# The last steps of the weight pieces, queued one by one on GpSimd ahead of the diagonal

## The chip, the core and the metric

The kernel runs on one core of one Trainium2 chip. The metric is the device time of the run in microseconds, lower is better. A core has five engines with a queue of their own each: TensorE (PE, matrix products), VectorE (DVE), ScalarE (ACT), GpSimd (POOL) and SyncE (SP, which issues the transfers here). Each engine works through its queue in the order in which the program issued it; between engines there are semaphores.

## The reference

Attention that keeps the 32 largest scores of each row, and behind it a two-layer block with a sigmoid-gated activation:

```python
B, H, S, D = 8, 8, 576, 64
scores = scale * np.matmul(q, k.transpose(0, 1, 3, 2))
kth = np.partition(scores, -32, axis=-1)[..., -32:-31]
scores = np.where(scores >= kth, scores, -1e9)
attn = softmax(scores)                    # with 1e-9 added to the sum
x = (attn @ v) -> (B*S, H*D)              # 4608 x 512
h = x @ w_in                              # 512 x 2048
out = (h / (1 + np.exp(-1.702 * h))) @ w_out   # 2048 x 512
```

`q`, `k`, `v` are float32. The two weight matrices are float64, and the kernel makes float32 of them on the chip.

## The kernel before

**Slots.** The attention is cut into `N` slots, 18 for each of the 8 batches: 128 query rows of two heads at a time (and slots for the rows left over). `slots` lists them. For a slot, TensorE makes scores (`scores`, L237), ScalarE copies them to SBUF (`copy_scores`, L248), VectorE finds the 32 largest of each row in four rounds of MAX8 (L257) and MATCH_REPLACE8 (L260) for each of two heads (`topk`, 14 operations). GpSimd makes the threshold `cut` (L276) and the shift `low` (L277) from it (`bounds`); ScalarE masks (L285) and takes exponentials (L288), whose sums are `den`. VectorE adds 1e-9 (`some`, L297) and takes the reciprocal (`rden`, L299). TensorE turns the probabilities round (`turn`, L319 and L322, later L317), ScalarE copies the result (`pt`, L327), TensorE multiplies by the values (L350).

**The division.** In the first eleven slots (`n < SETTLED`, 11) GpSimd writes a diagonal matrix `by` of the reciprocals (L303, two operations of 128x128), and the turn multiplies by it, so it divides on the way. `by` has one buffer (`dgp`): the diagonal of the next slot waits until the last turn that reads the one before is through. Later slots scale the probabilities themselves, one head on ScalarE (L305) and one on GpSimd (L306).

**The block behind.** 128 finished rows go through `hidden` (L400, with `win`), `tanh` (L417), `gate` (L433 on VectorE in the first slots, L430 and L431 on GpSimd later) and `project` (L448, with `wout`), which is issued from slot 8 on.

**The weights.** There are 32 pieces of 128x512 numbers, 16 of `w_in` and 16 of `w_out`. They come in during the first slots: 2 pieces belong to slots 0 and 1, 3 to each of slots 2 to 9, 2 to slots 10 and 11 (`by_slot`). Transfers into 8 buffers (`raws`) bring the float64 numbers as pairs of 32-bit words. Five steps make float32 of a piece: `size` (ScalarE, L147), `shift` (VectorE, L148), `low` (ScalarE, L150), `sign` (ScalarE, L149), and on GpSimd an integer addition (L143) and a multiplication by the sign (L144), called `finish`. `size`, `shift`, `low` and `sign` run in the piece's own slot; `finish` is put on the list `unfinished`, and `finish_one` issues it in the next slot.

**The order of the work.** The engines' queues are written by hand (`tc.manual_schedule()`): the order of the Python calls is the order on each engine. In `slot(n)` GpSimd gets `bounds(n - 1)`, then, between the operations of `topk(n)`, the entries of `unfinished` and `by` of slot n - 1 (`divide(n - 1)`, after the sixth operation of top-k). The turn of slot n - 1 is issued in slot n from `TURNS` (4) on; in slots 2 to 4 the turn of slot n - 2 is issued at the slot's start. From slot 12 on `two_slots` takes two slots at a time, and `find` issues one entry of `unfinished` after each operation of top-k from the third on. The list `finished` holds one entry for each finished piece, and `project` is issued only when its pieces are on it.

In the text a slot's number is the `n` of `slot(n)`, from 0; "the turn" is L319 and L322; "piece" is the GpSimd part of a piece (L143 and L144) where GpSimd's queue is spoken of.

Of the kernel before, what the change touches and what calls it, by code (L numbers as in the profile page):

```python
# [9 lines left out]
ALU = mybir.AluOpType  # L10
# [3 lines left out]
I32 = mybir.dt.int32  # L14
# [14 lines left out]
def kernel(  # L29
# [27 lines left out]
    nc = tc.nc  # L57
# [24 lines left out]
    TURNS = 4  # L82
# [44 lines left out]
    def round_piece(n):  # L127

        c, g = pieces[n]
        dst = wout[:, g, :] if c is None else win[:, c, g * PIECE : (g + 1) * PIECE]
        words = raw.pop(n)[:].rearrange("p (n w) -> p n w", w=2)
        low, high = words[:, :, 0], words[:, :, 1].bitcast(F32)
        bits, whole = dst.bitcast(U32), dst.bitcast(I32)  # L140

        def finish():
            nc.gpsimd.tensor_tensor(out=whole, in0=whole, in1=low.bitcast(I32), op=ALU.add)  # L143
            nc.gpsimd.tensor_tensor(out=dst, in0=dst, in1=high, op=ALU.mult)  # L144

        return {
            "size": lambda: nc.scalar.activation(dst, high, AF.Abs, scale=REBASE),  # L147
            "shift": lambda: nc.vector.tensor_scalar(bits, bits, 3, None, op0=ALU.logical_shift_left),  # L148
            "sign": lambda: nc.scalar.activation(high, high, AF.Sign),  # L149
            "low": lambda: nc.scalar.mul(out=low.bitcast(I32), in_=low, mul=2.0**-29),  # L150
            "finish": finish,
        }


# [89 lines left out]
    def copy_scores(n):  # L244
        ps = st[n].pop("ps")
        sc = st[n]["sc"] = scp.tile([P, 2, S], F32, name="sc")
        for i in range(2):
            nc.scalar.copy(out=sc[:, i, :].rearrange("p (c k) -> p c k", c=2), in_=ps[i][:, :, 0:HALF])  # L248

    def topk(n):  # L250

        sc = st[n]["sc"]
        top = st[n]["top"] = small.tile([P, 2, TOPK], F32, name="top")
        left = lefts.tile([P, 2, S], F32, name="left")

        def largest(r, i):
            nc.vector.max(top[:, i, 8 * r : 8 * r + 8], (left if r else sc)[:, i, :])  # L257

        def remove(r, i):
            nc.vector.match_replace(  # L260
                left[:, i, :], top[:, i, 8 * r : 8 * r + 8], (left if r else sc)[:, i, :], LOWEST
            )

        ops = []
        for r in range(TOPK // 8):
            ops += [lambda r=r, i=i: largest(r, i) for i in range(2)]
            if r < TOPK // 8 - 1:
                ops += [lambda r=r, i=i: remove(r, i) for i in range(2)]
        return ops

    def bounds(n):

        top = st[n]["top"]
        cut = st[n]["cut"] = small.tile([P, 2], F32, name="cut")
        low = st[n]["low"] = small.tile([P, 2], F32, name="low")
        nc.gpsimd.tensor_scalar(cut[:], top[:, :, TOPK - 1], -1.0, None, op0=ALU.mult)  # L276
        nc.gpsimd.tensor_tensor(out=low[:], in0=top[:, :, TOPK - 1], in1=top[:, :, 0], op=ALU.subtract)  # L277

    def exponentials(n, between=lambda: None):

        sc, cut, low = st[n]["sc"], st[n]["cut"], st[n]["low"]
        pr = st[n]["pr"] = prp.tile([P, 2 * S], F32, name="pr")
        den = st[n]["den"] = small.tile([P, 2], F32, name="den")
        for i in range(2):
            nc.scalar.activation(sc[:, i, :], sc[:, i, :], AF.Prelu, bias=cut[:, i : i + 1], alpha=HUGE)  # L285
        between()
        for i in range(2):
            nc.scalar.activation(  # L288
                pr[:, i * S : (i + 1) * S], sc[:, i, :], AF.Exp, bias=low[:, i : i + 1],
                accum_out=den[:, i : i + 1],  # L290
            )

    def divide(n):

        den, pr = st[n]["den"], st[n]["pr"]
        some = small.tile([P, 2], F32, name="some")
        nc.vector.tensor_scalar_add(some[:], den[:], 1e-9)  # L297
        rden = small.tile([P, 2], F32, name="rden")
        nc.vector.reciprocal(rden[:], some[:])  # L299
        if n < SETTLED:  # L300
            by = st[n]["by"] = dgp.tile([P, 2, P], F32, name="by")
            for i in range(2):
                nc.gpsimd.tensor_scalar(by[:, i, :], ident[:], rden[:, i : i + 1], None, op0=ALU.mult)  # L303
        else:
            nc.scalar.activation(pr[:, 0:S], pr[:, 0:S], AF.Copy, scale=rden[:, 0:1])  # L305
            nc.gpsimd.tensor_scalar(pr[:, S : 2 * S], pr[:, S : 2 * S], rden[:, 1:2], None, op0=ALU.mult)  # L306
# [22 lines left out]
    def turn_main(n):  # L329
        for i in range(2):  # L330
            turn(n, i * NF, MAIN[i], NF)

    def turn_ends(n):

        turn(n, 2 * NF, FULL, 1)
# [76 lines left out]
    def tanh(aside):  # L412

        if to_gate:
            ph, g, rows = to_gate.pop()
            th = thp.tile([P, G, P], F32, name="th")
            nc.scalar.activation(th[:], ph[:], AF.Tanh, scale=0.851 / RAISE)  # L417
            if aside:
                h = raws.tile([P, G, P], F32, name="h", tag="raw")
                nc.scalar.copy(out=h[:], in_=ph[:])  # L420
                ph = h
            gated.append((th, ph, g, rows))
# [65 lines left out]
    unfinished = []  # L488
    early = []
    finished = []  # L490

    def finish_one():
        unfinished.pop(0)()
        finished.append(None)

    def may_project(waiting):

        return len(to_project) > waiting and len(finished) >= NG * CC + (to_project[0][1] + 1) * G
# [63 lines left out]
    def bring_all():  # L562

        waiting = len(ready)
        while put_off:
            put_off.pop(0)()
        if len(ready) > waiting:
            hidden()

    def slot(n):  # L570

        todo = later.pop(n, [])
        for fn, args in todo:
            if fn is not prepare:
                fn(*args)
        preparing = [args for fn, args in todo if fn is prepare]
        some = [round_piece(x) for x in by_slot.get(n, [])] if n else early
        if n == 0:
            for piece in some:
                piece["low"]()  # L580
                piece["sign"]()
        else:
            bounds(n - 1)

            exponentials(n - 1, bring_all if n % 4 == 1 else lambda: None)
            copy_scores(n + 1)
            bring_all()
            while signs:
                signs.pop(0)()
            if 1 < n <= TURNS:  # L590
                turn_main(n - 2)
                turn_ends(n - 2)
            for piece in some:
                piece["size"]()
            tanh(False)
        for i, op in enumerate(topk(n)):
            op()
            if i == 2:
                for _ in range(min(1, len(unfinished))):
                    finish_one()  # L600
            if i == 5:
                if n > 0:
                    divide(n - 1)
                while unfinished:
                    finish_one()
            if i == 10:
                gate(False)
        for piece in some:
            piece["shift"]()
            unfinished.append(piece["finish"])  # L610
        if n < NP:
            for args in preparing:
                prepare(*args)
        if n >= TURNS:
            turn_main(n - 1)
            turn_ends(n - 1)
        if n > 0:
            for piece in some:
                piece["low"]()
        scores(n + 2)  # L620
        if n == SETTLED:
            copy_scores(n + 2)
        if n == 0:
            return
        for i, piece in enumerate(some):
            if n == TURNS and i > 0:
                signs.append(piece["sign"])
            else:
                piece["sign"]()
        idle = not ready and n < TURNS  # L630
        if 1 < n <= TURNS:
            values(n - 2, put_off if n == TURNS else None)
        if n >= TURNS:
            values(n - 1, put_off)
        if n >= NP:
            for args in preparing:
                prepare(*args)
        if n > PROJECTS and may_project(2):
            project(range(G))
        if idle:  # L640
            stay_warm(8)
        hidden()
# [118 lines left out]
```

## Time and profile before

| | |
|---|---|
| median of 4 runs | 1612.61 us (1612.29 to 1613.07) |
| the profiled execution | 1612.37 us |
| its span | 1610.6 us |
| PE busy | 1577.9 us (98%) |
| DVE busy | 1477.4 us (92%) |
| ACT busy | 1151.5 us (71%) |
| POOL busy | 745.8 us (46%) |
| one MAX8 or MATCH_REPLACE8, 128x576 | 743 to 747 ns |
| `raw` transfer, 512 KB | 3.4 and 5.1 us from issue to landing |

The page cuts the span into 40 slices of 40 us; a digit is an engine's busy share in tenths, and in the row PEclk the clock that TensorE was granted. The chain of waits follows the work that ended last back to the start, at each step to what released it. In timelines a row is the start, the duration, the engine, the line, the operation, what is written from what, and how many; in brackets the idle time of the engine before it and what ended it. Rows of like instructions are merged (x3), and a VectorE instruction's start there overlaps the end of the one before by about 0.08 us.

Two waits of TensorE in the first 110 us:

| row of the timeline | idle before, ended by |
|---|---|
| L319 at 59.60 us | 0.77 us, POOL `by` |
| L319 at 107.16 us | 2.60 us, POOL `by` |

### The profile page before, as it was taken

The page shows a single profiled execution, that of the slowest core. Times are in us where ns is not written, and L with a number is a line of the kernel's source. Part 1 is how long each engine was busy: PE and PEld are TensorE (multiplying, and loading weights), DVE is VectorE, ACT ScalarE, POOL GpSimd, SP SyncE. Part 2 cuts the span into 40 slices and gives each one's busy share as a digit, 9 for nine tenths or more (in the row PEclk, how much of TensorE's full clock was granted, in tenths as well). Part 3 has the DMA queues.
Part 4 walks back from the last instruction along what each step waited for, and adds up shares of the span by engine and source line. Part 5 has one row for each costly group of instructions (what it writes and reads, how often), then busy time and mean ns, then how long its engine had stood idle before and what let it go on. Part 6 is the DMA issues. An engine that isn't in the chain of part 4 may idle for free.

```text
span 1610.6 us, 32158 instructions
## 1 busy us (share of the span) xinstructions
PE 1577.9 (98%) x12045; PEld 1181.1 (73%) x12045; DVE 1477.4 (92%) x3218; ACT 1151.5 (71%) x2442; POOL 745.8 (46%) x780
## 2 busy tenths in 40 slices
PE   7789999999999999999999999999999999999999
PEld 5667777777777777777777777777777777777776
DVE  7999999999999989999999999999999999999960
ACT  7898776777776776677766777677767777777751
POOL 3877334444444434444444434444444444444430
PEclk8899999999999999999999999999999999999999
DMA  7451111010001001110001000001000100000000
GB/s 225 139 154 46 33 30 29 19 38 5 23 15 45 22 23 30 30 43 16 22 15 45 22 23 25 22 20 38 15 22 16 44 22 23 23 8 8 8 8 14
DMA packets 99100, 56.61 MB, mean 35 GB/s; under 512 B 81536, under 2 KB 90240, under 8 KB 98944
## 3 DMA queue, kind: packets, MB, share of 16 engines
q1 hardware_dynamic: 98512, 54.25, 12.1%
q8 instruction: 95, 1.56, 0.4%
q14 instruction: 61, 0.50, 0.1%
q10 hardware_dynamic: 432, 0.30, 0.1%
HBM read 45.09 MB, written 9.44 MB: 34 GB/s over the span
## 4 chain that ended last, share of the span: by engine, by line
PE 92%; DVE 6%; ACT 1%; issue 0%; POOL 0%; ACTq 0%; POOLq 0%
PE ph L400 32%; PE po L448 31%; PE s_ps L237 9%; PE o L350 9%; PE tp L317 8%; DVE top L257 3%; DVE left L260 2%; PE tp L205 2%; ACT sc L248 1%; PE tp L319 1%; DVE win L148 1%; PE none L165 0%; PE tp L211 0%; DVE wout L148 0%; ACT pr L305 0%
## 5 line engine op out<-in xcount | busy, mean ns | idle before, releaser
L257 DVE MAX8 top<-left 128x8 f32<-128x576 f32 x864 | 609.3, 747 | 0.0
L448 PE MATMUL po<-wout,gT 128*128 128x512 f32 x1152 | 540.2, 593 | 0.7 <-ACT ob L453 0.7
L400 PEld LDWEIGHTS ph<-xT,win 128*128 128x128 f32 x4096 | 467.8, 192 | 41.5 <-issue 41.0
L400 PE MATMUL ph<-xT,win 128*128 128x128 f32 x4096 | 484.6, 277 | 0.1
L260 DVE MATCH_REPLACE8 left<-top,left 128x576 f32<-128x576 f32 x576 | 423.4, 743 | 0.0
L306 POOL TENSOR_SCALAR pr<-pr,rden 128x576 f32<-128x576 f32 x133 | 229.5, 1726 | 349.9 <-ACT th L417 345.5
L448 PEld LDWEIGHTS po<-wout,gT 128*128 128x128 f32 x1152 | 197.9, 191 | 146.3 <-issue 144.6
L327 ACT COPY pt<-tp 128x512 f32<-128x512 f32 (+1 forms) x432 | 192.7, 481 | 150.6 <-PE tp L317 142.7
L430 POOL TENSOR_SCALAR th<-th 128x512 f32<-128x512 f32 x131 | 195.7, 1494 | 220.8 <-ACT th L417 220.8
L285 ACT ACTIVATE sc<-sc,cut 128x576 f32<-128x576 f32 x288 | 208.2, 774 | 120.6 <-POOL cut L276 118.6
L248 ACT COPY sc<-s_ps 128x576 f32<-128x576 f32 x288 | 169.8, 644 | 70.0 <-PE s_ps L237 69.7
L288 ACT ACTIVATE pr<-sc,low 128x576 f32<-128x576 f32 x288 | 219.2, 764 | 0.0
L317 PEld LDWEIGHTS tp<-ident,pr 128*128 128x128 f32 x1197 | 143.1, 141 | 102.0 <-issue 57.4
L260 DVE MATCH_REPLACE8 left<-top,sc 128x576 f32<-128x576 f32 x288 | 211.6, 742 | 0.0
L257 DVE MAX8 top<-sc 128x8 f32<-128x576 f32 x288 | 202.0, 743 | 2.2 <-ACT sc L248 2.2
L237 PE MATMUL s_ps<-k_t,q_t 64*128 64x288 f32 (+1 forms) x1280 | 182.2, 431 | 0.3 <-ACT k_t L207 0.3
L317 PE MATMUL tp<-ident,pr 128*128 128x128 f32 x1197 | 174.2, 273 | 0.0
L431 POOL TENSOR_TENSOR gT<-th,h 128x512 f32<-128x512 f32 x131 | 167.0, 1275 | 10.9
L350 PE MATMUL o<-pt,v_l 128*64 128x128 f32 (+1 forms) x2560 | 157.7, 266 | 0.7
L350 PEld LDWEIGHTS o<-pt,v_l 128*64 128x64 f32 x2560 | 130.4, 137 | 32.4 <-ACT pt L327 13.5
L237 PEld LDWEIGHTS s_ps<-k_t,q_t 64*128 64x128 f32 (+1 forms) x1280 | 99.4, 178 | 58.9 <-issue 41.4
L276 POOL TENSOR_SCALAR cut<-top 128x2 f32<-128x2 f32 x144 | 38.0, 264 | 206.8 <-DVE top L257 206.8
(66 smaller groups left out, 1174.3 us busy)
## 6 DMA issues: line engine op xcount, KB each, us to landing
q_l<-in_q_dram SPq DMA_DIRECT2D x64, 128.0 KB, 3.1
raw<-in_moe_w_in_dram SPq DMA_DIRECT2D x16, 512.0 KB, 5.1
v_l<-in_v_dram SPq DMA_DIRECT2D x32, 256.0 KB, 3.0
raw<-in_moe_w_out_dram SPq DMA_DIRECT2D x16, 512.0 KB, 3.4
out_dram<-ob SPq DMA_DIRECT2D x32, 256.0 KB, 2.3
k_l<-in_k_dram SPq DMA_DIRECT2D x62, 128.0 KB, 3.0
ends<-in_q_dram SPq DMA_DIRECT2D x32, 32.0 KB, 2.7
v_e<-in_v_dram SPq DMA_DIRECT2D x64, 16.0 KB, 2.5
```

Source lines behind the costliest of these rows:

```text
L237: nc.tensor.matmul(ps[i][rows, c, 0:HALF], lhsT=qT[b, hps[p]][on, cols], rhs=kT[b, hps[p]][on, FIRST[i] + c * HALF : FIRST[i] + (c + 1) * ...
L257: nc.vector.max(top[:, i, 8 * r : 8 * r + 8], (left if r else sc)[:, i, :])
L260: nc.vector.match_replace(left[:, i, :], top[:, i, 8 * r : 8 * r + 8], (left if r else sc)[:, i, :], LOWEST)
L285: nc.scalar.activation(sc[:, i, :], sc[:, i, :], AF.Prelu, bias=cut[:, i : i + 1], alpha=HUGE)
L288: nc.scalar.activation(pr[:, i * S : (i + 1) * S], sc[:, i, :], AF.Exp, bias=low[:, i : i + 1], accum_out=den[:, i : i + 1],)
L306: nc.gpsimd.tensor_scalar(pr[:, S : 2 * S], pr[:, S : 2 * S], rden[:, 1:2], None, op0=ALU.mult)
L317: nc.tensor.transpose(tp[:, c * P : (c + 1) * P], pr[:, at], ident[:])
L327: nc.scalar.copy(out=to, in_=tp[:, 0 : blocks * P])
L350: nc.tensor.matmul(o[j * D : (j + 1) * D, 0 : cols.stop - cols.start], lhsT=main[:, j, c, :] if c < NF else tail[:, j, :], rhs=pt[:, j * N ...
L400: nc.tensor.matmul(ph[:, i, :], lhsT=win[:, c, f * P : (f + 1) * P], rhs=xT[:, c, :], start=(c == 0), stop=(c == CC - 1),)
L430: nc.gpsimd.tensor_scalar(th[:], th[:], 1.0, None, op0=ALU.add)
L448: nc.tensor.matmul(po[:], lhsT=gT[:, i, :], rhs=wout[:, f, :], start=(f == 0), stop=(f == FC - 1))
```

## The change

Each piece leaves two entries on `unfinished` instead of one, the addition and the multiplication, and `finish_one` issues one of them. The count on `finished` moves into the multiplication. Ahead of `divide(n - 1)`, after the third operation of top-k, up to three entries are issued in slots 4 and on, and up to six in slots before; it was one piece, that is one addition and one multiplication, in every slot. What is left of the list follows `divide` as before. `find` is not edited; as it issues one entry per operation of top-k, in slot 12 it now issues three operations ahead of `divide` and one behind it, where it was two pieces ahead of it.

```diff
@@ round_piece
+        def add():
+            nc.gpsimd.tensor_tensor(out=whole, in0=whole, in1=low.bitcast(I32), op=ALU.add)
+
         def finish():
-            nc.gpsimd.tensor_tensor(out=whole, in0=whole, in1=low.bitcast(I32), op=ALU.add)
             nc.gpsimd.tensor_tensor(out=dst, in0=dst, in1=high, op=ALU.mult)
+            finished.append(None)
...
-            "finish": finish,
+            "finish": [add, finish],
@@ finish_one
     def finish_one():
         unfinished.pop(0)()
-        finished.append(None)
@@ slot
             if i == 2:
-                for _ in range(min(1, len(unfinished))):
+                for _ in range(min(3 if n >= TURNS else 6, len(unfinished))):
                     finish_one()
             if i == 5:
                 if n > 0:
                     divide(n - 1)
...
             piece["shift"]()
-            unfinished.append(piece["finish"])
+            unfinished.extend(piece["finish"])
```

## The prediction

> **What bounds the kernel now.** I read the shares of the chain of waits first, then the chain in order of time, then GpSimd's and VectorE's timelines in the first 110 us, then the granted clock in short windows. The profiled execution took 1612.37 us (span 1610.6).
>
> ```profile
> POOL 3877334444444434444444434444444444444430
> PEclk8899999999999999999999999999999999999999
> ...
> PE 92%; DVE 6%; ACT 1%; issue 0%; POOL 0%; ACTq 0%; POOLq 0%
> ```
>
> GpSimd (POOL), the only engine whose order changes, has no share of the chain. The 6% of VectorE (DVE) are all at the front. There the chain reads (start, duration, what):
>
> ```profile
> 40.00 1.00 DVE win L148 x3
> ...
> 50.91 2.61 DVE win L148 x3
> ...
> 63.44 2.63 DVE win L148 x3
> ...
> 76.62 1.40 DVE win L148 x3
> ...
> 88.53 1.43 DVE wout L148 x3
> ...
> 100.52 1.45 DVE wout L148 x3
> ...
> 106.50 0.61 POOL by L303
> 107.11 0.04 issue
> 107.16 3.68 PE tp L319 x16
> 110.84 0.37 PE tp L322 x4
> ```
>
> The reader should see one step with five prices. Three `shift`s (L148) cost 1.00 us at the end of slot 2 and 2.61, 2.63, 1.40, 1.43 and 1.45 at the ends of slots 3 to 7. Everything between them is top-k without a pause. At 107.16, in slot 8, the chain goes over to TensorE, which from 200 us on has no gap at all. So whatever the front gains or loses until 107.16 arrives whole at the end. GpSimd shows what makes the dear shifts:
>
> ```profile
> 46.38 1.18 POOL L303 TENSOR_SCALAR by<-ident,rden 128x128 f32<-128x128 f32 x2 [2.52 <-PE tp L322]
> ...
> 50.17 1.30 POOL L143 TENSOR_TENSOR win<-win,raw 128x512 int32<-128x512 int32 x1
> 51.55 1.35 POOL L144 TENSOR_TENSOR win<-win,raw 128x512 f32<-128x512 f32 x1
> 52.88 0.68 POOL L276 TENSOR_SCALAR cut<-top 128x2 f32<-128x2 f32 x1
> ```
>
> In slot 3 GpSimd waits 2.52 us for `by`'s buffer, and so its last piece still runs when the shifts begin at 50.84. The first shift ends at 51.76, 0.28 after the addition's end (51.48), the second at 53.19, 0.29 after the multiplication's end (52.90). A shift that meets a two-input GpSimd operation waits it out. `cut` is queued behind the same piece and comes 2 us after top-k's end at 50.91, and ScalarE's exponentials wait for it.
>
> **The change, part by part.** No instruction is added or taken away. The orders of TensorE, VectorE, ScalarE and SP stay, and with them every DMA issue. On GpSimd `by` (L303) moves behind its slot's second piece in slots 1 and 2 and behind all three in slot 3, and in slots 4 to 11 behind one more addition. In slot 12 the last multiplication goes behind the scaling of `pr` (L306).
>
> Slots 1 and 2: the second piece moves into the wait ahead of `by` (1.60 and 2.65 us). GpSimd was idle before `cut` here already (1.73 and 0.66), so nothing is gained. 0.
>
> Slot 3: additions and multiplications follow at 1.36 and 1.27 us (48.90 to 50.17), so a piece is 2.63. From 41.20 three end by 41.20 + 3 x 2.63 = 49.1, and `by` (1.18) by 50.3, before the shifts at 50.84. Their price falls from 2.61 to slot 2's 1.00: **-1.61**. `by` is 2.8 us later, but is read only by the turn at 51.92 in slot 4, 1.6 us on. Without that cover the excess would go onto ScalarE's copies, which wait for the turn.
>
> Slot 4: VectorE is 1.61 early throughout. `cut` is no longer late, and the exponentials start 1.11 after top-k's end (as 41.11 after 40.00), at 52.02 and not 53.59: 1.57 early. The turn whose end frees `by` follows them, so `by` starts at 58.95 - 1.57 = 57.38. Three operations are done by 56.0; the other three end 5.07 after `by`'s start (1.14 + 1.27 + 1.36 + 1.30), at 62.45. The first shift wants to start at 63.35 - 1.61 = 61.74 and still waits. At the end of slot 5 in the trace such a wait until 0.53 after the start made the price 1.40, 0.40 over; 0.71 makes it 1.58. **-1.05**.
>
> Slots 5 to 7: `by` waits for `rden`, with 1.85 to 2.04 us of idle time in front of it. One addition with its gap is 1.36 and fits. Three operations remain behind `by`: they end 5.07 after it, near 73.0 in slot 5, with top-k's end at 63.41 + 10.55 = 73.96. So each shift price falls to 1.00: **-0.40, -0.43, -0.45**. From slot 8 on the same happens beside a TensorE that is the bound: 0.
>
> Sum: 1.61 + 1.05 + 1.28 = 3.94 us by the start of slot 8's top-k. What ScalarE may keep back: its exponentials in slot 5 start 7.25 after slot 4's `by`, at 64.63, and their sums are there 3.26 later, at 67.89; VectorE wants them at 63.41 + 4.02 = 67.43 (70.09 less 66.07): 0.46 lost. `tanh` ends 7.64 after that start, at 72.27; the gate (L433) wants it at 71.6: 0.6 more. Together 1.1 us lost if TensorE's half clock in slot 4 stays as it is (59.5 to 62.8 at 0.50), about 0.1 if the earlier turn meets the full clock sooner. I take 0.2 to 0.3, because the 57.38 start leaves more busy time in the window before; both ends stay: 2.8 to 3.8. So **-3.7**.
>
> The small step `some` (L297) is the new meeting. In slots 1 to 11 it now comes up while a piece runs. Two rows show that:
>
> ```profile
> 153.64 0.70 DVE L297 TENSOR_SCALAR some<-den 128x2 f32<-128x2 f32 x1 [0.71 <-ACT pr L288]
> ...
> 184.03 0.50 DVE L297 TENSOR_SCALAR some<-den 128x2 f32<-128x2 f32 x1
> ```
>
> Alone it takes 0.15. At 153.64 a multiplication ran until 0.68 after its start; at 184.03 a one-input operation ran on for 1.36 and cost 0.35. In slots 2 to 7 it starts 4.68 (two pieces) or 5.02 (three) after the last top-k's end, and the second addition ends at 4.78 or 5.12: 0.1 later, about its own length. I take 0 each; the bounds are 0 and one more operation, 1.36.
>
> The Trainium skill, "SBUF — State Buffer", section "Who interferes with whom", speaks against the change: of a GpSimd and a two-port VectorE instruction the later one fully blocks until the first is through. Of the two rows 153.64 agrees; 184.03 does not, as `some` was done 1 us before the GpSimd operation. By the rule the sum would lose about 0.1 per slot, by the rows nothing.
>
> Slot 12: the multiplication (1.30) now stands between `pr` and the gate's two GpSimd steps (L430, L431). Before `cut` there was 0.93 idle, so `cut` is some 0.4 late. The `pr` that comes of it was scaled by 166.35 and is read by TensorE at 176.84, ten us on: 0. Without that cover, 0.4. The pieces' raw buffers come free up to 4 us earlier in slots 1 to 4 and 1.3 in later ones, so SP's loads behind them start no later: 0.
>
> **The clock at the hand-over.** TensorE ran slot 8's turn at half clock (PEclk in short windows; columns as in the page, PE first):
>
> ```profile
> 93.60:97.00 3.40, 1.80 (x16) 1.80 (x16) 3.37 (x9) 3.40 (x9) 2.44 (x3) 1.00 0.79 225
> 103.90:107.20 3.30, 0.70 (x7) 0.51 (x6) 3.27 (x11) 3.30 (x10) 1.29 (x3) 1.00 0.52 162
> 107.30:110.60 3.30, 3.30 (x16) 3.29 (x16) 3.30 (x8) 1.66 (x4) 3.22 (x4) 0.50 0.38 85
> ```
>
> A gap of 2.60 us before 107.16 left 0.70 busy in one window, and the next was at 0.50: the turn took 3.68 and not 1.79 as at 120.82. A gap of 1.75 (1.80 busy) kept the full clock. Slots of 11.55 instead of 11.95 make the gap about 2.2, between the two. The forecast keeps the half clock; the full one saves 1.89 more.
>
> The Trainium skill, "TensorE: Matmul & The Clock Gate", section "Why this matters for your kernels", asks for gaps of no more than about 3 us; by it slot 8 would not have been slow at all, which the 0.50 row contradicts. By the page the clock adds nothing to the sum; by the rows it adds up to 1.89.
>
> **The rivals.**
> *Full clock in slot 8:* 3.7 + 1.89 = 5.6 saved, 1606.8. For it: the shorter gap. Against: 2.2 is nearer to 2.60 than to 1.75.
> *ScalarE and the half clock keep more:* a slot with a half-clock turn goes from `by` to `by` in 11.99 (82.56 to 94.55), 0.44 over 11.55, whatever the shifts cost. With the 1.1 of slot 5 and two such slots, 3.94 - 1.1 - 0.88 = 2.0: 1610.4. For it: at 94.06 `some` waited for ScalarE already. Against: slots 5 and 7 ran at full clock.
> *No gain:* `by` still delays the last piece, or the shifts wait for something else: 1612.4. Against: the 0.28 and 0.29 us above.
> *Slower: `some` misses the gap between two operations* and is shut out for one more, 1.36, in each of slots 1 to 7: 9.5 lost, 3.9 gained, 1618. It decides from the third miss on (4.1). For it: in slots 1 to 3 a multiplication follows the addition at 0.07. Against: the shifts at 50.84 took just such a gap, and in slots 4 to 7 `by` follows, which itself waits for `some`.
>
> **How the numbers follow.** Forecast (0.45): 1612.37 - 3.7 = 1608.7; the median is 0.24 higher, inside the runs' spread of 0.8, so I leave it. Full clock 0.25; ScalarE 0.20; no gain 0.04; slower 0.06. The forecast's own range is 1608.3 to 1609.8 (3.8 and 2.8, with 0.3 of spread). The range goes from 1606.3 (5.6 and 0.5 of spread) to 1611.2, which leaves out no gain, slower and little else. 0.2%, which is about what a measurement can tell, lies at 1609.4. Faster: full clock and 0.42 of the forecast, 0.67; same: ScalarE, no gain and the forecast's last 0.03, 0.27; slower 0.06.
>
> **What would show it.** In the profile after: shifts of 1.00 at the ends of slots 3 and 5 to 7 and near 1.6 in slot 4; `by` with a wait for the turn left in slot 4 only; `cut` at top-k's end; slot 8's turn near 103.4; from there the same rows. A `some` over 0.3, a VectorE idle before `some` or the gate, or a slot 8 turn of 1.8 would each name the rival that came in.

## The result, and the profile after

| | before | after |
|---|---|---|
| median | 1612.46 us (54 runs, 1610.52 to 1613.81) | 1610.21 us (34 runs, 1608.00 to 1611.27) |
| the profiled execution | 1612.37 us, span 1610.6 | 1608.05 us, span 1606.2 |

By the medians 2.25 us are gained; the ratio of the times is 0.9983, with an interval of 0.9978 to 0.9988, which is 1.9 to 3.5 us. The 34 runs lie in groups: 7 between 1608.0 and 1608.6, 25 between 1609.9 and 1610.5, 2 near 1611.2. The profiled execution is one of the first group; a second profile (experiment `a1_again`, 1610.31 us) is of the large one. Both are read here.

VectorE's timeline of the changed kernel, the three shifts (now L151) at the ends of slots 3 to 7 (start, duration, engine, line):

```profile
50.44 1.08 DVE L151 TENSOR_SCALAR win<-win 128x512 uint32<-128x512 uint32 x3
...
61.34 1.39 DVE L151 TENSOR_SCALAR win<-win 128x512 uint32<-128x512 uint32 x3
...
73.84 1.08 DVE L151 TENSOR_SCALAR win<-win 128x512 uint32<-128x512 uint32 x3
...
85.36 1.08 DVE L151 TENSOR_SCALAR wout<-wout 128x512 uint32<-128x512 uint32 x3
...
96.86 1.07 DVE L151 TENSOR_SCALAR wout<-wout 128x512 uint32<-128x512 uint32 x3
```

These rows hold about 0.08 us that overlap the end of top-k. Without it the prices are 1.00, 1.31, 1.00, 1.00 and 0.99 us, where they were 2.61, 2.63, 1.40, 1.43 and 1.45. GpSimd's timeline of the same kernel shows why in slot 3:

```profile
47.39 1.30 POOL L146 TENSOR_TENSOR win<-win,raw 128x512 f32<-128x512 f32 x1
48.66 1.19 POOL L306 TENSOR_SCALAR by<-ident,rden 128x128 f32<-128x128 f32 x2
50.61 0.99 POOL L279 TENSOR_SCALAR cut<-top 128x2 f32<-128x2 f32 x1 [0.76 <-DVE top L260]
```

The last piece and `by` are done at 49.85, GpSimd waits 0.76 us for top-k, and `cut` starts with the shifts and not 2 us behind them. TensorE's timeline of the same kernel has what was not forecast:

```profile
91.63 2.87 PE L322 MATMUL tp<-by,pr 128*128 128x128 f32 x16 [2.36 <-POOL by L306]
...
103.14 2.05 PE L322 MATMUL tp<-by,pr 128*128 128x128 f32 x16 [1.34 <-POOL by L306]
105.64 0.44 PE L325 MATMUL tp<-by,pr 128*64 128x128 f32 x4 [0.45 <-ACT pt L330]
...
152.09 1.12 PE L451 MATMUL po<-wout,gT 128*128 128x512 f32 x2 [0.49 <-POOL wout L146]
```

Slot 8's turn (103.14) runs at the full clock; slot 7's, behind a gap of 2.36, now runs into the half clock (a window from 92.7 to 96.0 us stands at 0.50). At 152.09, in slot 12, TensorE waits for a multiplication of GpSimd.

Every profile of this study can be cut at three points: the first shift (end of slot 0's top-k), the start of slot 8's turn, and the product that follows the first output copy (L451, slot 12). What follows the last point is 1452.3 to 1452.4 us in all twelve, so a span is the sum of four numbers:

| profile | opening | front | middle | rest | span |
|---|---|---|---|---|---|
| before | 18.77 | 88.38 | 51.11 | 1452.32 | 1610.6 |
| after | 18.37 | 84.77 | 50.77 | 1452.33 | 1606.2 |
| `a1_again` (after) | 19.55 | 85.97 | 50.67 | 1452.33 | 1608.5 |
| `a2_first` | 19.28 | 86.78 | 50.89 | 1452.33 | 1609.3 |
| `a3_rest` | 18.97 | 87.30 | 51.81 | 1452.32 | 1610.4 |
| `a4_slot12` | 19.07 | 85.93 | 50.22 | 1452.35 | 1607.6 |
| `b1_fill4` | 19.32 | 84.29 | 51.06 | 1452.33 | 1607.0 |
| `b2_fillall` | 18.57 | 84.13 | 49.48 | 1452.34 | 1604.5 |
| `b3_fillbefore` | 18.68 | 88.23 | 51.13 | 1452.35 | 1610.4 |
| `b4_some` | 18.39 | 88.22 | 50.82 | 1452.34 | 1609.8 |
| `c1_four` | 19.29 | 84.02 | 49.51 | 1452.37 | 1605.2 |
| `c2_fillall` | 19.68 | 84.13 | 49.50 | 1452.33 | 1605.6 |

The opening is the same code in all of them and differs by up to 1.3 us. So the front and the middle are what the experiments are compared by, beside the medians.

### The profile page after: what moved, and what is told of

The parts are those of the page before. It is cut to its first block, busy times and chain, and to the rows that moved or that the text cites. A ratio compares the mean times of both kernels' runs of the same rounds, so it can differ in the third digit from the quotient of the medians.

```text
span 1606.2 us, 32167 instructions
## 1 busy us (share of the span) xinstructions
PE 1577.4 (98%) x12045; PEld 1179.6 (73%) x12045; DVE 1471.3 (92%) x3218; ACT 1151.5 (72%) x2442; POOL 746.7 (46%) x780
## 3 DMA queue, kind: packets, MB, share of 16 engines
q8 instruction: 95, 1.56, 0.4%
## 4 chain that ended last, share of the span: by engine, by line
PE 93%; DVE 4%; ACT 3%; POOL 0%; issue 0%; POOLq 0%; ACTq 0%
PE ph L403 32%; PE po L451 31%; PE o L353 10%; PE s_ps L240 10%; PE tp L320 8%; DVE top L260 2%; PE tp L208 2%; DVE left L263 1%; ACT sc L251 1%; PE tp L322 1%; ACT pr L291 0%; PE none L168 0%; ACT raw L152 0%; DVE win L151 0%; ACT pt L330 0%
## 5 line engine op out<-in xcount | busy, mean ns | idle before, releaser
L451 PE MATMUL po<-wout,gT 128*128 128x512 f32 x1152 | 540.5, 594 | 1.2 <-ACT ob L456 0.7
L451 PEld LDWEIGHTS po<-wout,gT 128*128 128x128 f32 x1152 | 197.8, 191 | 147.2 <-issue 144.1
```

The lines of the kernel that those rows point to most:

```text
L451: nc.tensor.matmul(po[:], lhsT=gT[:, i, :], rhs=wout[:, f, :], start=(f == 0), stop=(f == FC - 1))
```

## The experiments

**The changed kernel again (`a1_again`).** No edit.

> The changed kernel once more, for a second look at its profile beside the runs of this chip. Theory (T): the front is 3.5 to 4 us shorter up to slot 8's turn, and the runs fall into two groups about 2 us apart, by whether slot 8's turn is at half clock: near 1610.2 with half clock, near 1608.1 without. In a 1610 profile slot 8's turn takes about 3.7 us or its window stands at 0.50; in a 1608 profile it takes about 2. Slot 12 shows TensorE waiting some 0.5 us for the last multiplication on GpSimd in both. Rival (R1): the groups have another cause, and the 1610 profile has the turn at full clock. Rival (R2): the front itself is only 2 us shorter.

Measured: 1610.13 us (10 runs: 4 from 1607.97 to 1608.59, 5 from 1610.06 to 1610.49, one at 1611.17), ratio 0.9983 (0.9974 to 0.9992). In this 1610.31 profile slot 8's turn takes 2.05 us at the full clock, as in the 1608 profile. So the theory's cause of the groups falls and R1 holds. The front is 2.41 shorter than before, nearer to the 2 of R2 than to the 3.5 to 4 of the theory. It is 1.20 longer than in the 1608 profile, and all of that lies in slots 4 and 5. TensorE's and VectorE's timelines of `a1_again`:

```profile
58.59 3.79 PE L322 MATMUL tp<-by,pr 128*128 128x128 f32 x16 [0.76 <-POOL by L306]
...
69.14 0.17 DVE L300 TENSOR_SCALAR some<-den 128x2 f32<-128x2 f32 x1 [1.08 <-ACT pr L291]
...
73.57 0.69 DVE L436 SCALAR_TENSOR_TENSOR gT<-th,ph 128x512 f32<-128x512 f32 x1 [0.57 <-ACT th L420]
```

and the same three of the 1608 profile of the changed kernel:

```profile
57.39 2.77 PE L322 MATMUL tp<-by,pr 128*128 128x128 f32 x16 [0.77 <-POOL by L306]
...
66.77 0.17 DVE L300 TENSOR_SCALAR some<-den 128x2 f32<-128x2 f32 x1
...
71.18 0.69 DVE L436 SCALAR_TENSOR_TENSOR gT<-th,ph 128x512 f32<-128x512 f32 x1 [0.55 <-ACT th L420]
```

Slot 4's second turn takes 3.79 us in the one and 2.77 in the other. Behind it ScalarE's copies, its exponentials and its `tanh` come later, and VectorE waits 1.08 us for the sums and 0.57 for the gate, 1.65 together, where the other waits 0.55. The granted clock shows what differs. Short windows of `a1_again` (window; its length; busy time of PE, PEld, DVE, ACT and POOL with counts; PEclk; DMA share; GB/s):

```profile
57.70:61.00 3.30, 2.54 (x13) 2.41 (x12) 3.30 (x9) 2.36 (x6) 3.07 (x4) 0.50 0.26 102
61.10:64.40 3.30, 3.30 (x16) 2.46 (x17) 3.30 (x7) 2.13 (x6) 2.92 (x5) 0.50 0.58 184
64.50:67.80 3.30, 3.30 (x49) 2.79 (x46) 3.30 (x8) 3.04 (x7) 2.84 (x3) 1.00 0.35 133
```

and of the 1608 profile:

```profile
55.20:58.50 3.30, 1.55 (x14) 1.31 (x15) 3.27 (x9) 3.25 (x7) 2.19 (x4) 1.00 0.50 159
58.60:61.90 3.30, 3.30 (x18) 2.47 (x18) 3.30 (x8) 2.23 (x6) 3.22 (x4) 0.50 0.47 154
62.00:65.30 3.30, 3.30 (x50) 2.74 (x47) 3.30 (x9) 3.21 (x8) 3.22 (x5) 1.00 0.55 165
```

One half-clock window against two. In `a1_again` TensorE was 2.54 of 3.30 us busy at the half clock, and the next window stayed at 0.50; only a window without idle time was followed by 1.00. The idle time just ahead of the turn (0.76 and 0.77 us) is much the same in both; in `a1_again` it lies inside the first half-clock window, in the 1608 profile ahead of it.

**One part alone (`a2_first`, `a3_rest`).** Against the changed kernel:

```diff
- for _ in range(min(3 if n >= TURNS else 6, len(unfinished))):
+ for _ in range(min(2 if n >= TURNS else 6, len(unfinished))):   # a2_first
+ for _ in range(min(3 if n >= TURNS else 2, len(unfinished))):   # a3_rest
```

> All operations ahead of the diagonal in slots 1 to 3 alone; from slot 4 on one whole piece ahead of it, as before. T: slot 3's shifts cost 1.00 instead of 2.61, and slot 4's stay contended: by starts near 57.4, four operations behind it end near 63.8, the shifts cost about 2.6; slots 5 to 7 stay at 1.40. So 1.6 us of the gain, ratio about 0.9990, 1610.8 with half clock. If the gain is ScalarE's earlier exponentials in slot 4 and not the shifts, nearly the whole gain (2.2 or more) is here.

> Three operations ahead of the diagonal from slot 4 on alone; slots 1 to 3 as before (one whole piece). T: slot 3's shifts stay at 2.61; slot 4's fall from 2.63 by one operation to about 1.3 to 1.6; slots 5 to 7 fall from 1.40 to 1.00. 1.0 + 1.28 = 2.3 us less by slot 8, less what ScalarE keeps: ratio 0.9985 to 0.9993. If only slot 3 matters: 1.0000.

Measured: `a2_first` 1611.34 us, 0.9992 (0.9983 to 1.0001); `a3_rest` 1611.47 us, 0.9992 (0.9984 to 1.0001). By the fronts, of one profile each, against 88.38: 1.60 less with slots 1 to 3 alone, the size worked out for slot 3; 1.08 less with slot 4 and later alone. The sum, 2.68, lies between the 2.41 of `a1_again` and the 3.61 of the other profile. Single shifts of `a2_first` at slot 4's end took 0.97, 1.52 and 0.41 us: its earlier exponentials alone did not cheapen them, so the shifts are the gain and not only the earlier `cut`. One thing was not as expected there: slot 5's shifts fell to 0.41 each too, but VectorE waited 0.40 us for the gate in that slot, so nothing came of it. In `a3_rest` slot 3's stayed dear (0.77, 1.51, 0.41) and slots 5 to 7 were at 0.41 each. Its shifts together cost some 2.5 us less than before; in slot 5 VectorE waited 0.60 us for the sums and 0.57 for the gate, which is most of what is missing from the front. The two intervals reach 1.0001; the split is carried by the fronts.

**Slot 12 as before (`a4_slot12`).** The last multiplication goes ahead of the division again:

```diff
-                if i > 1 and unfinished:
-                    finish_one()
+                if i > 1:
+                    for _ in range(min(2, len(unfinished))):
+                        finish_one()
```

> The changed kernel, with both pieces of slot 12 ahead of the division again. T: TensorE's 0.49 us wait for the last multiplication in slot 12 is gone, everything before it is the same: 0.5 us less than the changed kernel, 1609.7 (half clock) or 1607.6. Rival: the wait moves on to the end of the one-buffer output copy or to ScalarE, and nothing is gained.

Measured: 1609.35 us, 0.9980 (0.9971 to 0.9989), 0.78 less than `a1_again` on the same chip. TensorE's timeline of `a4_slot12`:

```profile
150.93 3.60 PE L451 MATMUL po<-wout,gT 128*128 128x512 f32 x8
155.22 1.98 PE L451 MATMUL po<-wout,gT 128*128 128x512 f32 x4 [0.69 <-ACT ob L456]
```

All eight products run in one piece; the wait of 0.49 is gone, and from the transpose in front of them (L214) to the product after the output copy it takes 155.22 - 150.77 = 4.45 us, in `a1_again` 156.20 - 150.99 = 5.21. The theory holds, at 0.76 rather than 0.5: besides the wait, the eight products take 3.60 us in one piece and 2.74 + 1.12 = 3.86 in two.

**The idle time filled (`b1_fill4`, `b2_fillall`, `b3_fillbefore`).** `b1` and `b2` start from `a4_slot12`, `b3` from the kernel before:

```diff
                 turn_main(n - 2)
+                if n == TURNS:                    # b1, b2, b3
+                    stay_warm(10)
                 turn_ends(n - 2)
...
         hidden()
+        if TURNS < n <= PROJECTS:                 # b2, b3
+            stay_warm(6)
```

> a4 (slot 12 restored) with ten more products of the identity on TensorE in slot 4, between the early turn's two parts, where it stands idle for some 2.6 us. Theory (T2): in most executions of the changed kernel slot 4's second turn runs at half clock (3.8 us), ScalarE's copies and then VectorE's gate in slot 5 come 1.1 to 1.2 us late, and this is what the 1608 executions are spared. With the idle time filled the turn takes about 2 us in nearly all, and the time is 1.0 to 1.2 below a4: 1608.2. Rival: it is only the phase of the opening, and filling changes nothing (1609.4); or the fill itself delays the turn's second part and costs up to 1 us.

> b1 and six more products at the ends of slots 5 to 7, where TensorE is idle for 1.3 to 2.4 us. T2: slots 7 and 8 are at full clock too, ScalarE's copies no longer wait; another 0.3 to 1 us: 1607.3 to 1607.9. Rival: slot 8's turn waits for by and by for VectorE whatever the clock, so nothing over b1.

> The kernel before with the same fills. T2: VectorE's shifts set its front, and half clocks in slots 4 to 6 are hidden there; only slot 8's turn at full clock helps: 1.1 to 1.4 us, 1611.2. Rival: the clock is the larger part of the changed kernel's gain, and this alone gives 2 us or more, 1610.5 or less.

Measured: `b1_fill4` 1608.36 us, 0.9970 (0.9960 to 0.9981); `b2_fillall` 1606.68 us, 0.9962 (0.9949 to 0.9974); `b3_fillbefore` 1612.10 us, 0.9994 (0.9985 to 1.0003). With slot 4 filled its second turn takes 2.05 us, where it took 3.78 in `a4_slot12`, and the front falls from 85.93 to 84.29, by 1.64. Most of it are the two waits of slot 5 in `a4_slot12`, of which `b1_fill4` has neither:

```profile
68.56 0.17 DVE L300 TENSOR_SCALAR some<-den 128x2 f32<-128x2 f32 x1 [0.78 <-ACT pr L291]
...
72.98 0.69 DVE L436 SCALAR_TENSOR_TENSOR gT<-th,ph 128x512 f32<-128x512 f32 x1 [0.56 <-ACT th L420]
```

VectorE's and TensorE's timelines of `b2_fillall`:

```profile
67.00 0.14 DVE L300 TENSOR_SCALAR some<-den 128x2 f32<-128x2 f32 x1
...
70.75 0.68 DVE L436 SCALAR_TENSOR_TENSOR gT<-th,ph 128x512 f32<-128x512 f32 x1
...
102.70 2.05 PE L322 MATMUL tp<-by,pr 128*128 128x128 f32 x16 [1.57 <-POOL by L306]
104.68 0.44 PE L325 MATMUL tp<-by,pr 128*64 128x128 f32 x4
```

Neither step of VectorE waits, and slot 8's turn goes on without the 0.45 us for ScalarE. From slot 4 to the hand-over in slot 8 no window is at the half clock. The five runs lie within 0.8 us, and their median is 0.6 below the range that was expected. In `b1_fill4` slot 8's turn was slow again in the profile (2.59 us), which cost its middle 0.84 against `a4_slot12`; with slots 5 to 7 filled too the middle is 49.48.

On the kernel before the fill is worth 0.36 us by the medians of 1612.46 and 1612.10, and 0.76 against the runs of its own chip, with an interval that holds 1. The expected 1.1 to 1.4 was missed: its slot 8 turn still came 2.02 us after the last product and took 3.68, so this run does not price the full clock there. What it does show is that the front (88.23) hardly moved, though slot 6 now kept the full clock. That the shifts and not the clock are the larger part of the change's gain is shown by the table: in `a1_again` the front is 2.41 shorter and the middle 0.44. What the clock decides, by `b1_fill4`, is how much of the front's gain is kept.

**The small step behind a longer queue (`b4_some`).** Three operations of 128x2 put GpSimd's pieces some 0.8 us later in slots 1 to 3:

```diff
             if i == 2:
+                if 0 < n < TURNS:
+                    for _ in range(3):
+                        nc.gpsimd.tensor_scalar(spare[:], ident[:, 0:2], 1.0, None, op0=ALU.mult)
```

> The changed kernel with three small operations (128x2) on GpSimd ahead of the pieces in slots 1 to 3, which move the pieces some 0.6 us later there; nothing else reads them. If VectorE's small step in front of the reciprocal waits out a two-input GpSimd operation, it takes about 0.7 us in slots 1 to 3 instead of 0.15 and ends within 0.05 of the addition's end, and the front is 1.6 us longer. If it slips in beside the operation, it stays below 0.3 and the front is the same.

Measured: 1611.98 us, 0.9997 (0.9987 to 1.0007). VectorE's timeline of `b4_some` in slots 1 and 2:

```profile
23.15 0.91 DVE L301 TENSOR_SCALAR some<-den 128x2 f32<-128x2 f32 x1
...
34.48 0.91 DVE L301 TENSOR_SCALAR some<-den 128x2 f32<-128x2 f32 x1
```

and GpSimd's in slot 1:

```profile
22.75 1.28 POOL L143 TENSOR_TENSOR win<-win,raw 128x512 int32<-128x512 int32 x1
24.10 1.29 POOL L146 TENSOR_TENSOR win<-win,raw 128x512 f32<-128x512 f32 x1
```

The addition ends at 24.03, `some` at 24.06. It waited the addition out, and got in ahead of the multiplication at 24.10. In all three slots it took 0.91, 0.91 and 0.89 us. The front is 2.25 us longer than that of `a1_again`, three times the 0.75 us, and nearly the whole gain of the change is gone.

**Past the change (`c1_four`, `c2_fillall`).** `c2_fillall` is `b2_fillall` unchanged; `c1_four` adds

```diff
- for _ in range(min(3 if n >= TURNS else 6, len(unfinished))):
+ for _ in range(min(3 if n > TURNS else 4 if n == TURNS else 6, len(unfinished))):
```

> b2 with four operations, two whole pieces, ahead of the diagonal in slot 4 instead of three. The first shift at slot 4's end then meets no multiplication: it falls from 0.75 to 0.41 us, 0.34 less for VectorE. Against it the diagonal starts some 0.3 us later, as the fourth operation ends after the turn has freed its buffer, and slot 4's second turn with it. Theory: the two cancel, 1606.4 to 1606.9. Rival: VectorE alone sets the front, and the 0.34 shows: 1606.3.

> b2 once more, for the ratio to the kernel before on one chip beside c1: 1606.7, no execution above 1607.3.

Measured on one chip: `c1_four` 1606.68 us, 0.9964 (0.9951 to 0.9976); `c2_fillall` 1606.47 us, 0.9963 (0.9949 to 0.9976), its highest run 1607.45, 0.15 over what was expected. The first shift of slot 4 fell to 0.41 us, and slot 4's turn waited 1.03 us for `by` instead of 0.77; the fronts are 84.02 and 84.13. They cancel, as expected. `b2_fillall` is the version to keep: 1606.5 to 1606.7, some 3.5 us below the changed kernel.

## Why the prediction was right or wrong

The forecast was 1608.7 us, 3.7 below the profiled execution before. The median is 1610.2, 2.25 us less than before by the medians; that is within the wide range, but above the forecast's own 1608.3 to 1609.8.

- **What bounds the front: right.** The shifts were the price and GpSimd's two-input operations the cause (`a2_first`, `a3_rest`). From the first output copy on nothing was given back: the rest is 1452.3 to 1452.4 us in every profile.
- **Slot 3, -1.61: right.** 2.61 became 1.00; alone (`a2_first`) the front gave 1.60.
- **Slot 4, -1.05: right in kind, at most somewhat too small.** The shifts cost 1.31 in the 1608 profile and 1.34 in `a1_again`, 1.3 less than before; in `a4_slot12`, with the same order up to there, they cost 1.56, nearly the 1.58 worked out.
- **Slots 5 to 7, -1.28: right** as a price, 1.00, 1.00 and 0.99.
- **What ScalarE keeps back: mis-sized.** The prediction had both waits, before `some` and before the gate in slot 5, with 1.1 us if the half clock in slot 4 stayed and 0.1 if not, and took 0.2 to 0.3 "because the 57.38 start leaves more busy time in the window before". That step failed. In the 1610 profile the half clock stayed in spite of a window with 2.54 us busy, and the waits took 1.65 us; even in the 1608 profile the gate waited 0.55. With the idle time filled (`b1_fill4`) both waits were gone. Of the 3.94 worked out for the front, `a1_again`, of the large group, and `a4_slot12` got 2.4.
- **Slot 8's turn at half clock: wrong, for the better.** 2.2 was the gap worked out; it was 1.34, because slot 7's turn now ran into the half clock and its work ended later. The turn had the full clock in four of the five profiles of kernels with only GpSimd's order edited. In the fifth, `a3_rest`, slot 7's turn kept the full clock; there the gap was 2.20, as worked out, and slot 8's turn met the half clock (2.56 us). The prediction kept slot 7 as it was, at the full clock. But the 1.89 us of the rival were not there either: ScalarE, late from slot 7, held the turn's second part by 0.45 (0.67 in `a4_slot12`), and the middle fell by 51.11 - 50.22 = 0.89 (`a4_slot12`).
- **Slot 12, 0: wrong.** The step followed `cut` and the `pr` behind it, not the moved multiplication's own reader. It is the last block of `w_out`, and slot 12's `project` reads it: 0.76 us by the profiles, 0.78 by the medians.
- **`some`: right in place and price.** In the changed kernel it took 0.14 to 0.17 us in slots 1 to 11, and where an addition was running, that ended 0.08 to 0.11 after its start. `b4_some` shows how near the loss was: 0.8 us of delay on GpSimd costs 0.75 in each of three slots. It ended after one operation, so the rival's further 1.36 was not seen. In the row at 184.03 that the prediction read, `some` was through 0.86 us ahead of the one-input operation's end, not a full 1 us; the reading stands.
- **The rivals.** The time of the one that ScalarE and the half clock keep more, 1610.4, is nearest to the median, partly by luck. Its first term was at work, with 1.65 us of waits in slot 5 and not 1.1. Its second, 0.44 for each slot with a half-clock turn, was not there: in `a1_again` slots 6 and 7 went from `by` to `by` in 11.51 us each, though slot 7's turn ran into the half clock (2.74 us). The full clock in slot 8 and the loss in slot 12, which it did not have, roughly cancel (0.89 and 0.76).

The sum for `a1_again`: the opening +0.78, the front -2.41, the middle -0.44, together -2.07; its span is 1610.6 - 1608.5 = 2.1 shorter. The code of the opening is the same, so what the change itself gives in this profile is 2.85.

What stays open: what puts a run of the changed kernel into the one group or the other. The two profiles differ by 1.18 us in the opening and by 1.20 in slots 4 and 5, and the traces tie both to where the clock's windows lie against the kernel's start. The first record of the granted clock comes at 3.92 us in the 1608 profile and at 6.45 in `a1_again`, and over the twelve profiles the opening grows with it without exception, from 18.37 (3.92) to 19.68 us (6.74). Each half-clock stretch up to slot 12 begins a whole number of 3.41 us after that record. So the kernel meets the same windows in another place in every run, as its slot 4 did in the two profiles. No run sets that place, and one profile was taken of each, so that it sorts the runs 7 to 27 is argued and not shown.

## What to carry to other kernels

When two engines lock each other out, the price of an operation depends on what the other engine has in hand at that moment. Put the movable work into the other engine's waits, and work out where each short step then falls against it. For a moved step, list its own readers as well as what is queued behind it. And where TensorE has gaps of one to three microseconds and another engine waits behind it, try to fill them: here a gain for VectorE was partly lost through TensorE's clock and ScalarE, and idle products gave it back. On the kernel before, where VectorE did not wait for TensorE's work, the same products gave nothing that is clear of the noise.

## What the runs showed of the hardware that was not expected

- Half clock came in stretches of 3.41 us or multiples of it. A window of 3.3 us with 1.55 us of TensorE busy at the full clock was followed by the half clock, one of 3.4 with 1.80 was not. The way back took more: 2.54 of 3.30 busy at the half clock did not suffice, full windows did. Cut into the windows of 3.41 us in which the stretches lie, all twelve traces agree up to slot 12: at the full clock at most 1.72 us busy were followed by the half clock each time, 1.84 or more never; at the half clock up to 2.80 us busy were followed by another such window each time, and windows of 3.20 or more by the full clock, with one exception (3.38, in the 1608 profile). So the limit on the way down lies near half of the window, not at a window without work.
- The same opening took 18.37 to 19.68 us up to the first shift. TensorE's first sixteen products took 3.41 us in the shortest profile and 3.78 in `a1_again`, and the sixteen transposes of `k` after them 1.04 and 1.64: the half clock reached further into the work in the one than in the other, as the first clock records at 3.92 and 6.45 us say too.
- VectorE's small operation, shut out by a two-input GpSimd operation, came through 0.03 us after its end and ahead of the next, which was already in GpSimd's queue.
